# Two attention layers on one core: layer A's output projection as seven block products at the end, and log-sum rows copied by two engines

## The chip, the cores and the metric

The kernel runs on one core of a Trainium2 chip. The metric is the device time of one execution in microseconds (us). Times are given as the median of several runs. The profile is of one execution.

## The reference

Two independent attention layers, A and B, each with its own input `x` (2048 x 1024), `wqkv` (1024 x 3072) and `wo` (1024 x 1024), 32 heads of 32 columns. The two outputs are concatenated.

```python
# layer A: each query sees 8 keys, two positions apart
off = arange(8) * 2;  idx = pos[:, None] - off[None, :]      # masked where idx < 0
attn = softmax(where(mask, einsum(q, k[idx]) * Dh**-0.5, -1e9));  o = einsum(attn, v[idx])
out_A = o.reshape(2048, 1024) @ A_wo
# layer B: each query sees the 256 positions up to itself
p = softmax(where(mask, q @ k.T * Dh**-0.5, -1e9));  o = p @ v
out_B = o.reshape(2048, 1024) @ B_wo
```

All of it is float32.

## The kernel before, in words

**Units and groups.** Each layer's 2048 rows are cut into four units of 512 rows. Units 0 to 3 are layer B (called dense), units 4 to 7 layer A (windowed; the host splits A's rows into even and odd positions, so that its eight keys are neighbours). A unit has eight groups (`NG`) of four heads, 128 columns each. For each unit there are four kinds of matmul work in the "gemm" stream: `qk_items` (queries and keys of a group, 2 x 8 k-tiles), `v_items` (values, in three parts), and `o_items` (a block of 128 output columns of the projection, 8 k-tiles). The attention of a group comes between: `first`, `log_sum`, `rows`, `second` and `values` for the dense units, `window` for the others.

**Split precision.** Every matmul operand is split into a high part (rounded to the matmul's float32r format) and a low part (the rest), and a product is three matmuls (`TERMS`, L41): high x high, high x low, low x high. So one k-tile is three matmuls of 128x512, a projection block is 8 x 3 = 24, and a unit's projection is 8 blocks, 192 matmuls.

**The stream of operands.** `Stream` (L131) brings weights and activations from DRAM as raw tiles of 128x1024 float32 (512 KB). There are `NRAW` = 3 raw buffers. POOL's queue issues the loads (L159), in the order of a list of items. `parts` (L195) makes the high part by a copy on ACT or DVE (L201, L204) and the low part by DVE subtracts of 512 columns (L207). Split weights go to three `wpool` tiles, split activations to nine `xpool` tiles. A load is issued when the split of the item three places earlier ends. The matmul items call `split_to` at fixed k-tiles to ask for the next split.

**What sets the order.** All instructions are written out in an order decided while the kernel is built: a `Clock` (L44) keeps for each engine when it would be free by the planner's own durations, callbacks are put off to such times (`defer`), and the loop at L1060 always issues the item that is ready first: row items ("a"), second passes ("2"), first passes ("1"), or gemm. Engines then run their own instructions strictly in that order and wait on semaphores.

**The parts that the change touches.**
- The plan (L243 to L254): units 1 to 7 carry the eight `o` blocks of the unit before, two ahead of each of the groups 2 to 5 (`O_SLOTS`); the eight blocks of unit 7 stand at the end, the first four with their last k-tile put off (`TAIL`, L1038).
- `finish` (L817): the attention output of a group (PSUM, 128x512) is copied to a high part on ACT (L822) and a low part on DVE (L826), into one of ten `opool` tiles, where the projection reads it (L645).
- `o_items` (L622): matmuls at L645, PSUM copied out by ACT or DVE (L536, L539), stored by ACT's queue (L662).
- `log_sum` and `rows` (L878 to L909), dense units only: minus the log of each row's sum, for 128 queries x 16 (head, query block) pairs, is split and transposed by one matmul with the identity (L896), 32x128 into PSUM. `spread` then makes four tiles of 32x512, one for each head, by DVE multiplies with a broadcast mask `pick` of 32x16 (L902). They go to rows 96 to 127 of the query tile, and the second pass (L940) waits for them.
- `constants` (L305): POOL builds masks and `pick` (two selects at L322) before it issues its first load.

The PSUM ring of the gemm stream, `rg`, has three banks.

## Time and profile before

| what | us |
|---|---|
| median of 3 runs | 1831.32 |
| lowest, highest | 1831.26, 1832.84 |
| span of the profiled execution (first to last instruction) | 1830.6 |
| median less that span, taken as what lies around it | 0.7 |
| TensorE (PE) busy | 1807.8 |
| VectorE (DVE) busy | 1202.9 |
| ScalarE (ACT) busy | 889.4 |
| GpSimd (POOL) busy | 394.4 |

How to read it: a group row gives the line, engine and operation, output and input names, shape and count, then busy time, mean ns of one, and the engine's idle time just before it with what ended it. PEld is TensorE's weight load, which runs beside its matmuls. Matmuls overlap in the pipeline, so that the mean ns of one is longer than the step from one to the next. A row of the windows view gives, for a stretch of time, its length, then each engine's busy time with its count of instructions, the granted TensorE clock, the mean busy share of the 16 DMA engines, and GB/s. "To landing" is from a DMA's issue to its last byte.

### The profile page before, as it was taken

What the parts mean: (1) busy time and instruction counts of PE and PEld (TensorE: products, weight loads), DVE (VectorE), ACT (ScalarE), POOL (GpSimd) and SP (SyncE); (2) the same over time, 40 slices, a digit from 0 to 9 for tenths busy, and PEclk for the clock granted to TensorE, in tenths of its full rate; (3) what the DMA queues carried; (4) which work ended last, traced back from release to release, by engine and by line L of the source; (5) the groups of instructions that cost most, each with busy time, mean ns of one, the idle gap of its engine ahead of it and who ended that gap; (6) DMA issues with size and microseconds to landing.
All of it is one profiled execution on the core that took longest, in us unless ns stands there. A gap on an engine that the chain in (4) does not pass through costs nothing.

```text
span 1830.6 us, 38331 instructions
## 1 busy us (share of the span) xinstructions
PE 1807.8 (99%) x14826; PEld 1477.5 (81%) x14826; DVE 1202.9 (66%) x2694; ACT 889.4 (49%) x2254; POOL 394.4 (22%) x926
## 2 busy tenths in 40 slices
PE   9999999999999999999999999999999999999998
PEld 7787777888778888788887788888888788888887
DVE  6677886768867669777777564655547445655463
ACT  5556466565655655656555343433425234423331
POOL 3322323233242324332233200110001000100000
PEclk9999999999999999999999999999999999999999
DMA  8455665545656456455554343444334443534432
GB/s 242 121 138 139 176 164 150 170 121 160 164 155 164 136 151 183 125 157 141 141 142 130 110 135 116 152 143 130 119 115 143 133 138 108 162 107 128 127 104 83
DMA packets 109141, 257.43 MB, mean 141 GB/s; under 512 B 14496, under 2 KB 29856, under 8 KB 108960
## 3 DMA queue, kind: packets, MB, share of 16 engines
q0 software_dynamic: 41760, 152.06, 28.1%
q1 hardware_dynamic: 56832, 83.00, 17.6%
q10 hardware_dynamic: 10368, 19.93, 3.0%
q8 instruction: 117, 1.92, 0.5%
q14 instruction: 64, 0.52, 0.1%
HBM read 164.63 MB, written 23.07 MB: 103 GB/s over the span
## 4 chain that ended last, share of the span: by engine, by line
PE 92%; DVE 4%; DMA 2%; ACT 2%; issue 1%; SPq 0%; ACTq 0%; POOL 0%; DVEq 0%; POOLq 0%
PE g L518 37%; PE g L645 19%; PE g L583 17%; PE s L940 5%; PE s L857 5%; PE o L987 5%; PE s L711 2%; PE o L774 2%; DMA raw<-xs 1%; DVE w L207 1%; DVE s L862 1%; ACT s L867 0%; DMA qst<-nat 0%; DMA pbuf<-nat 0%; DVE x L207 0%
## 5 line engine op out<-in xcount | busy, mean ns | idle before, releaser
L518 PE MATMUL g<-x,w 128*128 128x512 f32 x3072 | 770.2, 394 | 3.8 <-DVE nm L729 2.4
L518 PEld LDWEIGHTS g<-x,w 128*128 128x128 f32 x3072 | 566.3, 189 | 114.2 <-issue 8.3
L583 PE MATMUL g<-w,x 128*128 128x256 f32 (+1 forms) x2304 | 391.9, 320 | 0.9 <-issue 0.7
L207 DVE TENSOR_TENSOR w<-raw,w 128x512 fp32r<-128x512 f32 x516 | 338.6, 698 | 52.0 <-ACT w L201 44.8
L583 PEld LDWEIGHTS g<-w,x 128*128 128x128 f32 x2304 | 332.3, 190 | 29.2 <-DVE w L207 1.8
L645 PE MATMUL g<-ot,w 128*128 128x512 f32 x1416 | 343.6, 393 | 3.7 <-DVE ot L826 1.8
L867 ACT ACTIVATE s<-s,nm 128x384 f32<-128x384 f32 (+2 forms) x512 | 274.3, 536 | 102.1 <-DVE nm L862 101.8
L862 DVE CUSTOM_DVE_ANT_0 s<-s,mask_d 128x384 f32<-128x384 f32 (+2 forms) x512 | 261.5, 553 | 88.2 <-PE s L857 87.5
L645 PEld LDWEIGHTS g<-ot,w 128*128 128x128 f32 x1416 | 262.4, 188 | 59.3 <-DVE ot L826 3.2
L926 POOL TENSOR_SCALAR_AFFINE_SELECT pbuf<-pbuf 128x128 f32<-128x128 f32 (+1 forms) x606 | 219.8, 391 | 325.1 <-ACT pbuf L947 323.8
L947 ACT ACTIVATE pbuf<-s 128x384 f32<-128x384 f32 (+2 forms) x480 | 202.7, 505 | 72.2 <-PE s L940 70.2
L159 POOL DMA_DIRECT2D raw<-wqk x126 | 68.1, 540 | 457.5 <-DVE w L207 356.3
L204 DVE CAST w<-raw 128x1024 fp32r<-128x1024 f32 x205 | 141.7, 691 | 24.8 <-PE g L518 24.0
L940 PEld LDWEIGHTS s<-qst,kst 128*128 128x128 f32 x704 | 113.0, 188 | 41.2 <-ACT s L867 16.3
L857 PE MATMUL s<-kst,qst 96*128 96x384 f32 (+2 forms) x512 | 142.4, 342 | 0.9 <-ACT s L867 0.6
L940 PE MATMUL s<-qst,kst 128*128 128x256 f32 (+2 forms) x704 | 136.5, 302 | 3.5 <-ACT s L867 3.0
L719 DVE TENSOR_TENSOR band<-s,near 128x160 f32<-128x160 f32 x128 | 32.4, 315 | 158.0 <-PE s L711 158.0
L536 ACT COPY ost<-g 128x512 f32<-128x512 f32 x54 | 31.7, 587 | 207.1 <-PE g L645 200.4
L857 PEld LDWEIGHTS s<-kst,qst 96*128 96x128 f32 x512 | 93.4, 189 | 26.2 <-issue 4.7
L826 DVE TENSOR_TENSOR ot<-o,ot 128x512 fp32r<-128x512 f32 x64 | 44.0, 688 | 101.6 <-ACT ot L822 101.4
L867 ACT ACTIVATION_READ_ACCUMULATOR s<-s,nm 128x1 f32 x512 | 105.3, 206 | 0.0
L159 POOL DMA_DIRECT2D raw<-wo x64 | 34.2, 534 | 304.2 <-DVE w L207 260.2
(77 smaller groups left out, 1298.6 us busy)
## 6 DMA issues: line engine op xcount, KB each, us to landing
raw<-wqk POOLq DMA_DIRECT2D x126, 512.0 KB, 4.3
raw<-wv POOLq DMA_DIRECT2D x72, 512.0 KB, 5.1
raw<-wo POOLq DMA_DIRECT2D x64, 512.0 KB, 4.1
qst<-nat SPq DMA_DIRECT2D x96, 256.0 KB, 5.3
kst<-nat SPq DMA_DIRECT2D x96, 256.0 KB, 5.6
raw<-xs POOLq DMA_DIRECT2D x28, 512.0 KB, 4.6
outs<-ost ACTq DMA_DIRECT2D x56, 256.0 KB, 2.3
kst<-halo SPq DMA_DIRECT2D x72, 128.0 KB, 4.5
```

What stands on the lines that cost most here:

```text
L159: (self.nc.scalar if early else self.nc.gpsimd).dma_start(raw if len(ap.shape) == 2 else raw.rearrange("p (a b) -> p a b", a=2), ap)
L204: nc.vector.tensor_copy(t[:, 0, :], raw)
L207: nc.vector.tensor_tensor(t[:, 1, c:c + 512], raw[:, c:c + 512], t[:, 0, c:c + 512].bitcast(F32), op=ALU.subtract)
L518: nc.tensor.matmul(h["ps"], h["w"][:, a, k * P:(k + 1) * P], xt[u][k][:, b, :], start=(k == 0 and i == 0), stop=(k == NK - 1 and i == 2))
L583: nc.tensor.matmul(ps, xt[u][kw * g + k][:, a, p0:p0 + P], h["w"][g][:, c, k], start=(first and t == 0 and half == 0), stop=(last and t == 2),
L645: nc.tensor.matmul(h["ps"], w[:, a, c:c + P], ot[u, k][:, b, :], start=(k == 0 and i == 0), stop=(k == NK - 1 and i == 2))
L857: nc.tensor.matmul(ps[:, :n], q[0:96, j, b * P:(b + 1) * P], kk[0:96, j, c0:c1], start=True, stop=True)
L862: nc.vector.tensor_tensor_reduce(ps[:, :n], ps[:, :n], mask[:, cut:full], scale=-1.0, scalar=BIG, op0=ALU.add, op1=ALU.min, accum_out=nm)
L867: nc.scalar.activation(ps[:, :n], ps[:, :n], AF.Exp, bias=nm, scale=-1.0, accum_out=sm)
L926: nc.gpsimd.affine_select(w, w, pattern=[[0, m], [step, n]], compare_op=ALU.is_ge, fill=0.0, base=base, channel_multiplier=chan)
L940: nc.tensor.matmul(ps[:, i * n:(i + 1) * n], kk[:, j, 256 + kb * P:256 + (kb + 1) * P], q[:, j, q0:q0 + n], start=True, stop=True)
L947: nc.scalar.activation(w, ps[:, :pack * n].rearrange("p (j n) -> p j n", j=pack), AF.Exp)
```

## The change

**Layer A's projection.** The units are taken in pairs (4 and 5, 6 and 7). With the two units as row blocks 1 and 2 of the left matrix, the halves of its columns as column blocks, and `wo` cut into 2 x 2 blocks of 512 x 512, the product of 2 x 2 blocks is formed from seven block products instead of eight. Each product has 4 output blocks of 4 k-tiles, 48 matmuls (L769).

- `finish` in units 4 to 7 copies the attention output to one plain tile on ACT (L1027), and SP stores it to DRAM (`od`, L1032).
- Sums and differences of blocks are made in the background: of the weights (`td`) after unit 3's last projection block, of the attention outputs (`sd`) when groups 4 to 7 of the second unit of a pair end. A task loads 2 x 512 KB on SP, does four DVE operations of 128x512, and stores 2 x 512 KB on SP. There are 4 weight tasks and 8 output tasks.
- All 14 products stand at the end of the gemm stream. Each has four items in the `Stream`: two of activations (`od` or `sd`), two of weights (`wo` or `td`).
- Each product's blocks are copied (first product, ACT) or added (DVE, L787) into running sums in SBUF; the results are stored from ACT's queue in the second, fifth, sixth and seventh product, those of the second and fifth through the one `ost` tile.
- The projection blocks of unit 3 (layer B) are spread over units 4 and 5, four in each (`O_LATE`). No projection stands in units 6 and 7.
- The ten `opool` tiles become a shared pool of ten tiles for attention outputs, background sums and running sums.

**Log-sum rows.** The split values are written with a stride into a zeroed tile `turn`, four matmuls (L1124) put query block b at columns 128b of PSUM, and each of the four copies is then one multiply with a per-row scalar, `pick` being 32x4. Each copy goes to ACT or DVE, whichever the planner has free first. `pick` is built by 32 selects of one column.

The core of the diff:

```diff
-    plan += [("o", U - 1, n) for n in range(NG)]
+    plan += [("p", u, i) for u in range(DU, U, 2) for i in range(7) if u > DU or i not in O_AT.values()]
+PRODUCTS = (("11", "11"), ("12", "21"), (0, 3), (2, 2), ("22", 1), (3, 0), (1, "22"))
+O_LATE = {4: {2: (0, 1), 3: (2, 3)}, 5: {2: (4, 5), 3: (6, 7)}}
...
+        def run(n, k):
+            if k == 0:
+                h["ps"], h["b"] = rg.take()
+            w, x = held["t", u, i, n // 2][0], held["s", u, i, k // 2][0][k % 2]
+            c = S * (n % 2) + P * k
+            for t, (a, b) in enumerate(TERMS):
+                nc.tensor.matmul(h["ps"], w[:, a, c:c + P], x[:, b, :], start=(k == 0 and t == 0),
+                                 stop=(k == 3 and t == 2))
+            if k == 1:
+                at = where["p", u, i, "t", 1]
+                more_w = [kind for kind, _ in st.items[at + 1:at + 1 + (n + 1 if n else 0)]]
...
+            if i == 0:
+                nc.scalar.copy(a, ps)
+            elif i == 1:
+                e = add(o, a)
+                store(0, 0, o, e)
...
+            elif i == 5:
+                e = add(c, c)
+                store(1, 1, c, e)
+                e = add(a, a)
...
+        if u >= DU:
+            o = slot(2 + hg % 2)[:, :S]
+            nc.scalar.copy(o, h["o"])
+            def store():
+                nc.sync.dma_start(od[u][:, s, :], o)
...
-            nc.tensor.matmul(ps[0:32, 0:P], hl.rearrange("p a b -> p (a b)"), cst["ident"], start=True, stop=True)
+            for b in range(4):
+                nc.tensor.matmul(ps[0:32, b * P:b * P + P], turn[:, 32 * b:32 * b + 32].bitcast(F32R), cst["ident"],
+                                 start=True, stop=True)
...
-                    nc.vector.tensor_tensor(q[96:P, j, :].rearrange("p (b s) -> p b s", s=P),
-                                            ps[0:32, None, 0:P].to_broadcast([32, 4, P]),
-                                            cst["pick"][0:32, 4 * j:4 * j + 4, None].to_broadcast([32, 4, P]), op=ALU.mult)
+                    if ck.ends("act", 0.62, ck.now) <= ck.ends("dve", 0.61, ck.now) + SPREAD:
+                        nc.scalar.activation(q[96:P, j, :], ps[0:32, :], AF.Copy, scale=cst["pick"][:, j:j + 1])
+                    else:
+                        nc.vector.tensor_scalar(q[96:P, j, :], ps[0:32, :], cst["pick"][:, j:j + 1], None, op0=ALU.mult)
...
-        for row in (0, 16):
-            nc.gpsimd.affine_select(pick, pick, pattern=[[-1, 16]], ...)
+        for row in range(0, 32, 4):
+            for b in range(4):
+                c = row // 4 % 4
+                nc.gpsimd.affine_select(pick[:, c:c + 1], pick[:, c:c + 1], pattern=[[0, 1]], ...)
+        nc.gpsimd.memset(turn, 0.0)
```

## The prediction

> **What bounds the kernel now.** I read the page's shares first, then the stretches of each stage, then the chain of work at the end.

> ```profile
> span 1830.6 us, 38331 instructions
> PE 1807.8 (99%) x14826; PEld 1477.5 (81%) x14826; DVE 1202.9 (66%) x2694; ACT 889.4 (49%) x2254; POOL 394.4 (22%) x926
> PE 92%; DVE 4%; DMA 2%; ACT 2%; issue 1%; SPq 0%; ACTq 0%; POOL 0%; DVEq 0%; POOLq 0%
> ```

> TensorE is busy 1807.8 of 1830.6 us, and the chain that ended last is TensorE for 92%. Only 22.8 us of the span are open to anything that is not TensorE work. Stage by stage (TensorE busy is the second number; then its count, weight loads, DVE, ACT, POOL, granted clock, DMA share, GB/s):

> ```profile
> 0.00:60.00 60.00, 56.84 (x233) 44.44 (x234) 39.68 (x101) 33.32 (x81) 18.55 (x49) 0.97 0.69 202
> 60.00:1030.00 970.00, 961.49 (x5895) 776.47 (x5896) 722.79 (x1854) 562.84 (x1627) 298.63 (x737) 1.00 0.54 148
> 1030.00:1780.00 750.00, 743.68 (x8436) 619.94 (x8431) 422.26 (x710) 281.99 (x526) 75.08 (x138) 1.00 0.43 130
> 1780.00:1827.00 47.00, 45.76 (x269) 36.63 (x267) 18.19 (x31) 10.70 (x20) 2.12 (x4) 1.00 0.26 84
> ```

> TensorE idles 3.2 us in the start, 8.5 in the dense layer, 6.3 in the windowed one, 1.2 at the end, and 3.6 after its last matmul. So the change is worth what it takes from the matmul stream, less the waits it puts in.

> **The matmuls removed.** Layer A's projection is 4 units x 8 blocks x 24 = 768 matmuls of 128x512 before. After it is 2 pairs x 7 products x 48 = 672 of the same shape. The pace stands in the chain's last pieces:

> ```profile
> 1805.13 21.77 PE g L645 x96
> 1826.90 0.02 issue
> 1826.92 0.58 ACT pbuf L536
> ```

> 96 matmuls took 21.77 us, 0.2268 each, and 96 is the number that goes: **-21.8 us**. They are taken from the engine that bounds, so nothing hides the gain. After the last matmul an eviction and a store remain, as before (0.69 instead of 0.58 us): 0.

> **The log-sum rows.** The 32 calls of `rows` make four matmuls instead of one, 96 more. `spread` shares 128 copies between two engines: the built order has 62 on DVE and 66 on ACT.

> ```profile
> 157.64 0.47 PE s L857 x4
> 160.33 0.06 PE s L896
> L896 PE MATMUL s<-ident,hl 128*32 128x128 f32 x32 | 7.1, 222 | 3.6 <-DVE hl L888 3.6
> L902 DVE TENSOR_TENSOR qst<-s,pick 32x512 fp32r<-32x512 f32 x128 | 79.3, 676 | 9.9 <-PE s L896 9.4
> ```

> In the chain one such matmul costs 0.06 us (its 222 ns are pipelined length). Four other 128-column matmuls in a row cost 0.47, or 0.12 each. I take 0.06, the row of the same shape: 96 x 0.06 = **+5.8 us**, at most 96 x 0.12 = 11.5. Nothing hides it. The gate of the second pass comes earlier: four DVE copies in a row were 2.7 us, two on each engine are 1.4. DVE loses 66 x 0.676 = 45 us of its 723 in the dense stage and ACT gains about as much on 563. That helps only where TensorE idles, 8.5 us in all. I take **-2 us**, between -5 and +3 (ACT is also in the softmax chain).

> **The start.** `pick` is now built by 32 selects of one column instead of two of 16, and one more memset follows, ahead of POOL's first load.

> ```profile
> 1.49 0.45 POOL L322 TENSOR_SCALAR_AFFINE_SELECT pick<-pick 32x16 f32<-32x16 f32 x2
> 10.02 1.19 POOL L159 DMA_DIRECT2D raw<-wqk  x2 [0.30 <-issue]
> 19.72 0.69 DVE L459 SCALAR_TENSOR_TENSOR nat<-g,nat 128x512 fp32r<-128x512 f32 x1 [4.46 <-ACT nat L455]
> 20.32 0.68 DVE L204 CAST w<-raw 128x1024 fp32r<-128x1024 f32 x1
> raw<-wqk POOLq DMA_DIRECT2D x126, 512.0 KB, 4.3
> ```

> At 0.19 to 0.225 us each, 30 more selects and a memset are 6 to 7 us. The first load goes out at 16 to 17 instead of 10.0, and with 4.3 us to landing arrives at 20.3 to 21.3. DVE split it at 20.3 anyway, since it stood behind L459. So the cover is used up: **+0.5 us**, between 0 and 1.5.

> **The end, where the new waits are.** Each product takes 48 x 0.2268 = 10.9 us and needs four raw tiles of 512 KB, two of activations and two of weights. Before, a block of 5.4 us needed one. The tiles pass through the same three raw buffers, POOL's load queue, ACT's high parts and DVE's low parts:

> ```profile
> q0 software_dynamic: 41760, 152.06, 28.1%
> outs<-ost ACTq DMA_DIRECT2D x56, 256.0 KB, 2.3
> L207 DVE TENSOR_TENSOR w<-raw,w 128x512 fp32r<-128x512 f32 x516 | 338.6, 698 | 52.0 <-ACT w L201 44.8
> L207 DVE TENSOR_TENSOR x<-raw,x 128x512 fp32r<-128x512 f32 x70 | 47.1, 692 | 16.6 <-ACT x L201 15.3
> L201 ACT CAST w<-raw 128x1024 fp32r<-128x1024 f32 x52 | 54.1, 1047 | 10.9 <-PE g L583 6.4 <-ACT ost L536 2.7 <-DVE band L731 0.7
> L201 ACT CAST x<-raw 128x512 fp32r<-128x512 f32 x31 | 17.8, 618 | 22.7 <-DMA raw<-xs 19.9 <-DVE x L204 2.6
> L539 DVE COPY pbuf<-g 128x512 f32<-128x512 f32 x2 | 1.4, 690 | 6.6 <-PE g L645 6.5
> ```

> DVE per product: 8 subtracts of 0.69 and 4 adds from PSUM (nearest row: the copy from PSUM, 0.69) are 8.3 us, and in the sixth product, with 8 adds, 11.0 of 10.9. The bank ring lets an add come 5.4 us late, so that passes. ACT's copies are 4 x 0.62 + 2 x 1.05 = 4.6.

> The three buffers are the tight loop. Counted from a product's start, splits for the next product are asked for after 18, 30 and 42 matmuls: 4.1, 6.8 and 9.5 us. The first activation tile's low parts end at 4.1 + 0.62 + 2 x 0.69 = 6.1 and free its buffer. The last weight tile is then loaded into that buffer and lands L later. It is split in 1.05 + 1.40 and frees the buffer at 8.55 + L. The following product's first weight tile goes there, and is split at 11.0 + 2L. TensorE needs it at 2 x 10.9 = 21.8. So L may be 5.4 us, and 5.2 with about 0.1 for each of four hand-overs. Beyond that **each product waits L - 5.2**.

> What L will be depends on the traffic:

> ```profile
> raw<-wo POOLq DMA_DIRECT2D x64, 512.0 KB, 4.1
> 1811.00:1816.00 5.00, 5.00 (x24) 4.14 (x23) 0.83 (x2) 0.19 (x1) 0.00 (x0) 1.00 0.14 52
> 700.00:740.00 40.00, 38.78 (x260) 29.54 (x259) 33.70 (x88) 23.53 (x65) 14.96 (x30) 1.00 0.72 204
> DMA to landing us min/median/max: 4.0/5.5/6.9
> 90.00:100.00 10.00, 10.00 (x79) 8.80 (x78) 8.26 (x28) 7.16 (x28) 0.55 (x1) 1.00 0.83 202
> DMA to landing us min/median/max: 4.8/4.8/4.8
> 20.00:44.00 24.00, 24.00 (x111) 19.34 (x109) 19.32 (x50) 14.15 (x33) 3.43 (x5) 1.00 0.99 263
> DMA to landing us min/median/max: 4.3/7.0/9.3
> ```

> A load holds the 16 engines 0.281 x 1830.6 / 290 = 1.77 us; a 256 KB store 0.14 x 5 = 0.7. A product without stores uses 7.1 of 10.9 us (65%). The second, fifth, sixth and seventh also store four blocks: 9.9 of 10.9 (91%). Loads land in 4.8 to 5.5 us at shares of 0.83 and 0.72, and in 7.0 at 0.99. At 91% I take 5.6, nearer to the former: 0.4 us in each of seven such products. The first pair is worse. While products 0 to 2 run, 12 loads (21.2), 4 stores (2.8), the last two sum tasks (each 2 x 1.77 in and 2 x 1.4 out, 12.7) and two attention stores (1.4) want 38.1 of 32.7 us. Of the 5.4 too many I charge 3, since the splits run a product ahead. Together **+6 us**; the bounds are 0 (L of 4.1 to 5.2) and 14 x (7.0 - 5.2) = 25.

> [...]

> **The windowed units.** Units 6 and 7 lose the projection blocks that stood between windows; unit 4 and 5 keep the dense layer's. From a window's scores to its values TensorE must have other work:

> ```profile
> 1737.13 1.32 PE L711 MATMUL s<-pbuf 32*32 32x40 f32 x128
> 1752.97 1.18 PE L774 MATMUL o<-wide,vbuf 128*32 128x8 f32 x40
> ```

> This one took 14.6 us after its scores. In the new order 48 matmuls and the next scores stand between, 12.1 us. But the windows lose 32 low parts of 0.69 on DVE, and the weight splits of layer A's blocks move to the end, so the vector chain is less disturbed. SP gets 32 attention stores and the sums' 48 transfers, in front of which seat copies for later windows wait. I take **+1 us** on the 6.3 now lost, between -3 and +10.

> **Sum.** 1830.6 - 21.8 + 5.8 - 2 + 0.5 + 6 + 1 = 1820.1. The median is 0.7 above the profiled span, so **1820.8 us**. About 0.2% (3.7 us) is what a measurement of this kernel can tell from no change.

> **Rivals.** The first row is for the third of them: least, median and greatest ns of POOL's load issues in the whole run.

> ```profile
> L159 POOL DMA_DIRECT2D raw<-wo x64: 528/528/651, 234.2 to 1797.6; - x64
> ```

> 1. *The raw-buffer loop takes the gain back* (slower). Without the end's waits the net gain is 16.5 us. Over 14 products that is 1.18 each, so it decides at L = 6.4. At the 7.0 of the start it costs 25 us: 1840. For it: 91% traffic in bursts. Against: stores come evenly spaced, and 4.8 at a share of 0.83. 0.11.
> 2. *No waits at the end.* Landing stays at 4.1 to 5.2, and +6 falls away: 1815. The median of 4.1 speaks for it, the 91% against. 0.20.
> 3. *The load queue is held up by DVE.* Each load's issue waits for a two-input subtract, 0.69 us. L is then 5.5 without stores and 6.3 with: 0.3 x 6 + 1.1 x 7 instead of 2.8, 7 us more, 1828. If it waits for both halves, 1834. [...] The row is against it: the issues take 528 ns in the median and 651 at most, with DVE two thirds busy. 0.06.
> 4. *The windows of units 6 and 7 run dry.* Half of the 2.5 us between 14.6 and 12.1, in some ten windows: 12 us, 1832. 0.07.
> 5. *The row matmuls don't pipeline.* 96 x 0.222 = 21 instead of 5.8: 1836. 0.04.
> 6. *The change doesn't do what it says.* The built order holds 672 product matmuls and 128 row matmuls, so this leaves only an unseen block: 0.02, slower.

> **How the numbers follow.** The forecast has 0.50 (1816 to 1827). Faster: forecast 0.50, rival 2 0.20, the lighter rival 3 and part of rival 1 below its point 0.07, together 0.77. Within 0.2%: rival 4 and the heavier rival 3, 0.08. Slower: rivals 1, 5, 6 and the worst of 4, 0.15. The range is 1810 (rival 2 with -5 in the dense stage) to 1836 (the row matmuls at 0.12 with 13 us at the end, or rival 5); some 0.13 is left out, most of it rival 1.

> **What would show it.** The product group (672 matmuls) should keep 0.2268 us in unbroken runs. Idle TensorE in the last 160 us should be about 6 us beyond its final 3.6, put down to DVE's low part of w at product starts, mostly in the first three products. The loads landing there should have a median of 5 to 5.6. POOL's first load should be at 16 to 17 us and row matmuls should cost 0.06 in the chain. The forecast is wrong if the windows of units 6 and 7 show idle TensorE above 10 us, or if loads take over 6.4 us.

## The result, and the profile after

The changed kernel takes 1900.35 us (median of 4 runs, 1896.20 to 1900.99), the kernel before 1831.29 beside it: a ratio of 1.037, 95% interval 1.036 to 1.039. The forecast was 1820.8, with a range of 1810 to 1836. The time went up by 69 us, where some 10 less were expected.

The profiled execution after is the shortest of the four (1896.20). Its page, with span and busy times:

```profile
span 1894.5 us, 38848 instructions
PE 1832.6 (97%) x14826; PEld 1481.9 (78%) x14826; DVE 1226.6 (65%) x2727; ACT 971.4 (51%) x2366; POOL 424.1 (22%) x979
```

TensorE now idles 61.9 us, before 22.8. The changed kernel has 21.8 us less product work and 5.8 more for the row matmuls, and yet TensorE is busy 24.8 us longer: part of its work ran at a lower clock. The stages of after, with the columns as in the rows of before (TensorE's granted clock is the third number from the end):

```profile
0.00:60.00 60.00, 50.00 (x199) 38.67 (x199) 35.06 (x87) 29.18 (x69) 22.18 (x66) 0.94 0.66 193
60.00:1070.00 1010.00, 987.24 (x5954) 787.85 (x5955) 690.49 (x1802) 607.93 (x1696) 306.93 (x745) 0.99 0.50 141
1070.00:1712.00 642.00, 631.39 (x7954) 525.52 (x7956) 388.56 (x658) 269.66 (x507) 65.91 (x118) 0.99 0.53 169
1712.00:1891.00 179.00, 163.94 (x726) 129.89 (x722) 112.46 (x182) 64.62 (x95) 29.07 (x51) 0.96 0.70 228
```

A clock of 0.99 over 1010 us looks harmless, and is 10 us or more. To see it I cut both traces into stretches of 2 us, and took from each its idle time (length less busy) and its clock loss (busy time by one less the granted clock). What is left I call work. (In the run e11 below, the lengths of the trains of matmuls give 16.9 us lost to the clock between 306 and 620 us; reckoned in this way from the granted clock, 0.93 up to 480 us and 0.95 behind it, they are 16.7.) The stages end at landmarks: the first first pass, the last second pass, the last window scores, the end. Each entry is idle / clock loss, in us:

| stage | length before, after | before | after | more |
|---|---|---|---|---|
| start | 31.1, 38.2 | 3.0 / 1.6 | 9.9 / 1.7 | 7.0 |
| dense | 995.3, 1028.7 | 8.7 / 0.0 | 22.8 / 14.6 | 28.7 |
| windows | 750.2, 641.8 | 6.3 / 0.0 | 8.5 / 3.3 | 5.5 |
| end | 54.0, 185.8 | 4.8 / 0.0 | 20.7 / 5.8 | 21.7 |
| sum | 1830.6, 1894.5 | 22.8 / 1.6 | 61.9 / 25.4 | 62.9 |

So 39.1 us more are idle and 23.8 are lost in clock. Work is almost as before (1807.2 against 1806.1), where 16.0 less were due. The other 17 us lie in time that counts as busy, for which the views list no wait. Four places carry the loss. The two largest:

**The dense stage.** The copies of the log-sum rows in after's timeline (start, duration, engine, operation, and in brackets the idle time before it with what ended it):

```profile
413.86 0.40 PE L1124 MATMUL s<-ident,turn 128*32 128x128 f32 x4
...
414.10 2.36 PE L650 MATMUL g<-w,x 128*128 128x256 f32 x18
414.30 0.74 DVE L1136 TENSOR_SCALAR qst<-s,pick 32x512 fp32r<-32x512 f32 x1 [1.00 <-PE s L1124]
415.08 0.68 ACT L1133 ACTIVATE qst<-s,pick 32x512 fp32r<-32x512 f32 x1 [2.55 <-DVE qst L1136]
415.79 0.74 DVE L1136 TENSOR_SCALAR qst<-s,pick 32x512 fp32r<-32x512 f32 x1 [0.75 <-ACT qst L1133]
...
416.57 0.68 ACT L1133 ACTIVATE qst<-s,pick 32x512 fp32r<-32x512 f32 x1 [0.81 <-DVE qst L1136]
...
417.30 1.03 PE L1172 MATMUL s<-qst,kst 128*128 128x128 f32 x6 [0.38 <-ACT qst L1133]
```

The four copies run one behind the other, 414.30 to 417.25: 2.95 us, not 1.4. While one engine copies the other stands, and six matmuls of the second pass wait for the last copy (0.38 us). The two groups, with idle time before them and what ended it:

```profile
L1136 DVE TENSOR_SCALAR qst<-s,pick 32x512 fp32r<-32x512 f32 x62 | 45.8, 743 | 45.6 <-ACT qst L1133 27.3 <-PE s L1124 18.1
L1133 ACT ACTIVATE qst<-s,pick 32x512 fp32r<-32x512 f32 x66 | 43.6, 675 | 93.1 <-DVE qst L1136 81.2 <-PE s L1124 11.5
```

ACT stood 81.2 us for DVE's copies and DVE 27.3 for ACT's. In the timeline each copy starts 0.03 to 0.04 us after the other engine's copy before it has ended, and that copy is named as what released it.

**The end.** What waited behind 1712 us (total us, times, longest), TensorE first, then DVE:

```profile
PE g L769 <- DVE ost L787: 12.1, 6, 6.2
```

```profile
DVE ost L787 <- DMA outs<-ost: 30.6, 11, 7.3
```

And the longest of them in the timeline:

```profile
1741.51 0.69 DVE L787 TENSOR_TENSOR ost<-g,r 128x512 f32<-128x512 f32 x1 [2.23 <-DMA outs<-ost]
...
1750.67 0.69 DVE L787 TENSOR_TENSOR ost<-g,r 128x512 f32<-128x512 f32 x1 [7.26 <-DMA outs<-ost]
...
1751.50 2.04 PE L769 MATMUL g<-x,w 128*128 128x512 f32 x4 [6.22 <-DVE ost L787]
1751.77 1.66 ACT L214 CAST x<-raw 128x512 fp32r<-128x512 f32 x3 [13.02 <-DVE ost L787]
```

There is one `ost` tile. An addition into it waits until the store before it has landed. The PSUM bank stays taken, and TensorE stops. ACT, whose queue holds the next store's issue in front of the casts, stands 13.0 us.

### The profile page after: what moved, and what is told of

Read it like the earlier page. It is cut to its first block, busy times and chain, and to the rows that moved or that the text cites. A ratio compares the mean times of both kernels' runs of the same rounds, so it can differ in the third digit from the quotient of the medians.

```text
span 1894.5 us, 38848 instructions
## 1 busy us (share of the span) xinstructions
PE 1832.6 (97%) x14826; PEld 1481.9 (78%) x14826; DVE 1226.6 (65%) x2727; ACT 971.4 (51%) x2366; POOL 424.1 (22%) x979
## 5 line engine op out<-in xcount | busy, mean ns | idle before, releaser
L582 PE MATMUL g<-x,w 128*128 128x512 f32 x3072 | 775.6, 397 | 7.0 <-ACT x L214 2.7
L582 PEld LDWEIGHTS g<-x,w 128*128 128x128 f32 x3072 | 572.4, 190 | 122.9 <-issue 5.8
L650 PEld LDWEIGHTS g<-w,x 128*128 128x128 f32 x2304 | 336.9, 192 | 28.7 <-issue 2.7
L1092 ACT ACTIVATE s<-s,nm 128x384 f32<-128x384 f32 (+2 forms) x512 | 274.2, 536 | 105.1 <-DVE nm L1087 103.9
L1158 POOL TENSOR_SCALAR_AFFINE_SELECT pbuf<-pbuf 128x128 f32<-128x128 f32 (+1 forms) x604 | 226.7, 407 | 291.4 <-ACT pbuf L1179 288.7
L710 PE MATMUL g<-r,w 128*128 128x512 f32 x768 | 196.7, 396 | 0.0
L769 PE MATMUL g<-x,w 128*128 128x512 f32 x672 | 162.0, 401 | 14.3 <-DVE ost L787 12.1
L769 PEld LDWEIGHTS g<-x,w 128*128 128x128 f32 x672 | 128.6, 194 | 47.5 <-issue 15.3
L710 PEld LDWEIGHTS g<-r,w 128*128 128x128 f32 x768 | 141.7, 188 | 28.4 <-issue 0.4
L1082 PE MATMUL s<-kst,qst 96*128 96x384 f32 (+2 forms) x512 | 149.6, 347 | 11.5 <-ACT s L1092 5.0
L1172 PE MATMUL s<-qst,kst 128*128 128x256 f32 (+2 forms) x704 | 143.9, 312 | 12.4 <-ACT qst L1133 7.5
L217 DVE CAST w<-raw 128x1024 fp32r<-128x1024 f32 x183 | 125.9, 688 | 32.6 <-PE g L582 19.9
L1082 PEld LDWEIGHTS s<-kst,qst 96*128 96x128 f32 x512 | 94.5, 190 | 40.2 <-ACT s L1092 13.2
L214 ACT CAST w<-raw 128x1024 fp32r<-128x1024 f32 (+1 forms) x77 | 79.5, 1037 | 61.6 <-DMA raw<-wo 19.9
L170 POOL DMA_DIRECT2D raw<-wv x72 | 46.2, 642 | 276.0 <-DVE w L220 172.1
## 6 DMA issues: line engine op xcount, KB each, us to landing
raw<-wqk POOLq DMA_DIRECT2D x126, 512.0 KB, 4.1
raw<-wv POOLq DMA_DIRECT2D x72, 512.0 KB, 4.3
qst<-nat SPq DMA_DIRECT2D x96, 256.0 KB, 3.7
kst<-nat SPq DMA_DIRECT2D x96, 256.0 KB, 4.0
raw<-wo POOLq DMA_DIRECT2D x44, 512.0 KB, 4.1
raw<-xs POOLq DMA_DIRECT2D x28, 512.0 KB, 6.0
outs<-ost ACTq DMA_DIRECT2D x48, 256.0 KB, 2.3
```

The costliest lines, as they stand in the source:

```text
L217: nc.vector.tensor_copy(t[:, 0, :], raw)
L582: nc.tensor.matmul(h["ps"], h["w"][:, a, k * P:(k + 1) * P], xt[u][k][:, b, :], start=(k == 0 and i == 0), stop=(k == NK - 1 and i == 2))
L650: nc.tensor.matmul(ps, xt[u][kw * g + k][:, a, p0:p0 + P], h["w"][g][:, c, k], start=(first and t == 0 and half == 0), stop=(last and t == 2),
L710: nc.tensor.matmul(h["ps"], w[:, a, c:c + P], ot[u, k][:, b, :], start=(k == 0 and i == 0), stop=(k == NK - 1 and i == 2))
L769: nc.tensor.matmul(h["ps"], w[:, a, c:c + P], x[:, b, :], start=(k == 0 and t == 0), stop=(k == 3 and t == 2))
L1082: nc.tensor.matmul(ps[:, :n], q[0:96, j, b * P:(b + 1) * P], kk[0:96, j, c0:c1], start=True, stop=True)
```

## The experiments

Medians, and ratios to the kernel before, measured beside it (1830.7 to 1832.3):

| kernel | us | ratio, 95% interval |
|---|---|---|
| changed kernel | 1900.35 | 1.0357 to 1.0387 |
| e1_two_banks | 1863.54 | 1.0154 to 1.0191 |
| e2_strassen_alone | 1846.08 | 1.0065 to 1.0097 |
| e3_logsum_alone | 1883.68 | 1.0267 to 1.0301 |
| e4_short_pick | 1890.01 | 1.0292 to 1.0351 |
| e6_spread_dve | 1875.28 | 1.0219 to 1.0249 |
| e8_strassen_pbuf | 1834.27 | 0.9996 to 1.0023 |
| e9_all_mended | 1848.23 | 1.0066 to 1.0100 |
| e10_spaced | 1834.16 | 1.0006 to 1.0030 |
| e12_fourth_raw | 1824.35 | 0.9955 to 0.9979 |
| e13_raw_spaced | 1824.40 | 0.9953 to 0.9977 |
| e14_told | 1893.46 | 1.0306 to 1.0361 |
| e15_dve_told | 1874.71 | 1.0205 to 1.0241 |

My theory at the outset: separate waits at the four places, each with clock lost behind it. The rival: one part of the change disturbs the other.

### Each part alone

**e2_strassen_alone** has the log-sum part and `pick` of the kernel before, from the first line to the copies:

```diff
-                hl = turn[:, :132].rearrange("p (b x) -> p b x", x=33)
+                hl = small.tile([P, 2, 16], F32R, tag="hl", name="hl")
...
-            for b in range(4):
-                nc.tensor.matmul(ps[0:32, b * P:b * P + P], turn[:, 32 * b:32 * b + 32].bitcast(F32R), cst["ident"],
-                                 start=True, stop=True)
+            nc.tensor.matmul(ps[0:32, 0:P], hl.rearrange("p a b -> p (a b)"), cst["ident"], start=True, stop=True)
```

> The changed kernel with the log-sum part and the constants of the kernel before (one row matmul, four VectorE products, pick of 32x16 with two selects): the Strassen part alone. Theory: start and dense stage are as before, first first-pass matmul near 31 us and last dense second pass near 1027, so 7 + 33 us less: 1856 to 1864, and what is left above before, 25 to 33 us, lies in the windows and at the end. Rival: the dense stage's loss comes with the Strassen part (dense products moved, tiles shared); then 1880 or more.

Measured: 1846.1, less than either theory gave. The dense stage is as before (996.8 us long, idle 7.7, clock 1.6). So its loss does not come with the projection.

**e3_logsum_alone** is the other half: the kernel before with the changed constants, row matmuls and copies.

```diff
-        pick = cst["pick"] = pickp.tile([32, 16], F32, name="pick")
+        pick = cst["pick"] = pickp.tile([32, 4], F32, name="pick")
...
-                hl = small.tile([P, 2, 16], F32R, tag="hl", name="hl")
+                hl = turn[:, :132].rearrange("p (b x) -> p b x", x=33)
```

> The kernel before with the changed constants and log-sum part alone (32 selects, four row matmuls, copies on two engines from one bank), layer A's projection classical. Theory: start +7 and dense stage +33 as in the changed kernel, nothing after: 1866 to 1874, that is slower than before by itself. Rival: the parts disturb each other, and alone this one costs less than 20 us: under 1852.

Measured: 1883.7, 52 us above before, more than expected; I had left out the matmul work that the dense stage leaves over for the windows. The two parts alone cost 14.6 and 52.2, together 66.8, where the change costs 69. They add up, so the rival falls. Three quarters of the loss is the log-sum part.

### The dense stage

**e1_two_banks** keeps everything but the bank:

```diff
-            ps, bank = rs.take()
+            halves = [rs.take() for _ in range(2)]
             for b in range(4):
-                nc.tensor.matmul(ps[0:32, b * P:b * P + P], ...)
+                ps = halves[b // 2][0]
+                nc.tensor.matmul(ps[0:32, b % 2 * P:b % 2 * P + P], ...)
...
+                    for d in range(2):
+                        ps = halves[d][0][0:32, 0:256]
+                        to = q[96:P, j, 256 * d:256 * d + 256]
+                        if d:
+                            nc.scalar.activation(to, ps, AF.Copy, scale=cst["pick"][:, j:j + 1])
...
+                        else:
+                            nc.vector.tensor_scalar(to, ps, cst["pick"][:, j:j + 1], None, op0=ALU.mult)
```

> The changed kernel, but the four transposed 128-column blocks go to two PSUM banks, two to each, and each engine copies the half that lies in its bank: VectorE four 32x256 copies with columns 0 to 255, ScalarE four with 256 to 511, none of them waiting for the other engine. As many row matmuls as in the changed kernel. Theory: the dense stage's 33 us come from the two engines taking turns at one bank (0.74 + 0.04 + 0.68 + 0.03 us, in series 3.0 us where the prediction had 1.4) and from the clock lost behind the stalls. Then the last dense second pass ends 25 to 34 us earlier than at 1066.9, the stage's idle time and clock loss fall to before's or less, and the time is 1866 to 1876. Rival: the four row matmuls, the turn tile or the Strassen part's tile layout slow the dense stage; then the time stays within 6 us of 1900.

Measured: 1863.5, 36.8 less and a little more than expected. The last second pass is at 1040.3 (26.6 earlier). The dense stage's idle time and clock loss fall to 12.9 and 5.1 us, not to before's 8.7 and 0.0 as expected. Four copies on each engine, and their groups, in this kernel:

```profile
402.60 1.65 DVE L1140 TENSOR_SCALAR qst<-s,pick 32x256 fp32r<-32x256 f32 x4 [0.88 <-PE s L1125]
402.72 1.53 ACT L1137 ACTIVATE qst<-s,pick 32x256 fp32r<-32x256 f32 x4 [1.77 <-PE s L1125]
```

```profile
L1140 DVE TENSOR_SCALAR qst<-s,pick 32x256 fp32r<-32x256 f32 x128 | 52.9, 470 | 21.1 <-PE s L1125 20.9
L1137 ACT ACTIVATE qst<-s,pick 32x256 fp32r<-32x256 f32 x128 | 49.0, 452 | 36.6 <-PE s L1125 36.2
```

Neither engine waits for the other any more, though both still read `pick` and write the same query tile. Only the row matmuls hold them. So it is the shared PSUM bank that made them take turns (81.2 and 27.3 us of waits for each other in after, none listed here). Four copies of 256 columns took 1.5 and 1.7 us here, side by side. The second bank has a price: TensorE's row matmuls now wait 3.9 us (five times) for a bank that ACT's exponentials still read (`PE s L1125 <- ACT s L1092`), a wait that the changed kernel does not have.

**e6_spread_dve.** Are the hand-overs the price, or the length of the series?

```diff
-SPREAD = 0.0
+SPREAD = -99.0
```

> The changed kernel with all four copies of the rows on VectorE (2.97 us in series by 0.743 each) and none on ScalarE; row matmuls, selects and projection as in the changed kernel. Theory: what costs is not the 3.0 us of the series but that each engine's queue stands behind the other at every hand-over, so that ScalarE's exponentials and VectorE's mask steps behind the copies start late. Without hand-overs the dense stage is as before plus the row matmuls (5.8) and 0.3 us a step (9): its last second pass at 1046 to 1054, the time 1880 to 1888. Rival: the length of the series and the dearer copies are the cost; then the series is as long as it was, and the time stays within 6 us of 1900 or rises, VectorE having 64 copies more.

Measured: 1875.3, 25 less, but the last second pass is at 1062.1 and the dense stage idles 22.6 us, as with hand-overs (22.8). So my theory, that the idle time is the price of the queues behind the hand-overs, fails. The four copies in a row are 2.72 us in its timeline, so the hand-overs had added only 0.2 us to the series. What fell is the clock loss (14.6 to 4.9), and time that counts as busy (the table below).

**e14_told** and **e15_dve_told.** The order of instructions is fixed by a planner that reckoned with 0.61 and 0.62 us for a copy and two engines side by side. Both kernels tell it the truth (e14 takes turns, j odd on ACT; e15 keeps `SPREAD` at -99, so that all copies go to DVE):

```diff
-                    if ck.ends("act", 0.62, ck.now) <= ck.ends("dve", 0.61, ck.now) + SPREAD:
+                    if j % 2:
...
-                        ends.append(ck.use("act", 0.62, ck.now))
+                        last = ck.use("act", 0.72, last)
...
-                        ends.append(ck.use("dve", 0.61, ck.now))
+                        last = ck.use("dve", 0.78, last)
```

> The changed kernel with the four copies still from one bank and in turn, VectorE, ScalarE, VectorE, ScalarE, but with the planner told so: 0.78 and 0.72 us each, one behind the other (3.0 us), where it had reckoned with two engines side by side (1.25 us). Theory A, the order: second passes were put into TensorE's queue 1.7 us too early, and TensorE, which can't pass them, stood; told, it is given other matmuls meanwhile, the dense stage's idle time falls from 22.8 to 10 to 16 us, the clock loss from 14.6 to under 6, and the time is 1867 to 1882. Theory B, the queues: whatever the plan, each engine stands at every hand-over with its own work behind it, and the time stays within 6 us of 1900.

> The changed kernel with all four copies on VectorE, as in e6_spread_dve (1875.3), and with the planner told 0.78 us for each (it took 0.61 there; the copies take 0.743). Theory A, the order: the second pass was planned 0.5 us too early, so some of the 22.6 us of idle time in the dense stage goes: 1862 to 1871. Theory B: the idle time there comes from VectorE's load (64 copies more than the changed kernel), which is as it was: 1872 to 1879.

Measured: 1874.7 in e15, as theory B had it, and 1893.5 in e14, 6.9 below the changed kernel and nearer to B than to A. TensorE's waits in the dense stage, first of after, then of e14:

```profile
PE s L1172 <- ACT qst L1133: 7.5, 19, 0.8
PE s L1082 <- ACT s L1092: 5.0, 6, 1.2
PE s L1172 <- DVE qst L1136: 3.9, 7, 1.5
PE s L1124 <- DVE turn L1115: 2.0, 1, 2.0
```

```profile
PE s L1124 <- DVE turn L1115: 9.3, 4, 2.9
PE s L1082 <- ACT s L1092: 4.8, 5, 1.3
PE s L1172 <- DVE qst L1136: 1.9, 2, 0.9
...
PE s L1172 <- ACT qst L1133: 0.8, 3, 0.3
```

Told the truth, the second pass no longer waits for the copies (11.4 us become 2.7), and TensorE waits for the split rows instead (2.0 become 9.3). The dense stages compared with before's 995.3 us, with the matmuls that were put off to the windows (57 of 512 columns and 6 of 256 in after, 42 of 512 in e1) charged at 0.2268 each, those of 256 columns at half of it:

| kernel | longer | put off | loss | of it idle | of it clock |
|---|---|---|---|---|---|
| changed | 33.4 | 13.6 | 47.0 | 14.1 | 14.6 |
| e14_told | 37.6 | -2.7 | 34.9 | 11.5 | 9.7 |
| e6_spread_dve | 29.4 | 0.0 | 29.4 | 13.9 | 4.9 |
| e15_dve_told | 28.5 | 0.7 | 29.2 | 8.5 | 6.7 |
| e1_two_banks | 6.8 | 9.5 | 16.3 | 4.2 | 5.1 |
| e2_strassen_alone | 1.5 | 0.0 | 1.5 | -1.0 | 1.6 |

Of the 47, some 12 go when the planner is told (but e14 loses them again in the windows, with 14.8 us idle and 11.0 of clock there). Another 19 go when the copies run side by side from two banks. How much of these 19 is the hand-overs and how much the length of the series is not separated: with a series of 2.72 us on one engine (e15), 6 of them go, and there VectorE does 64 copies more than in e14. The last 16 stay: 5.8 for the row matmuls, the rest idle time and clock. Nor is the shared bank all of it. e6 has, as before, all copies on VectorE, in 2.72 us where before has 2.48, and still loses 29.4, of which the row matmuls are 5.8. Of the other 24, 13.9 are idle time and 4.9 clock: TensorE waits there for ACT's exponentials (`PE s L1082 <- ACT s L1092` 8.4 us, in before 0.6) and for the split rows (7.7, before 3.6). Why these come later than in before is not shown. And before's 8.7 us of idle time in this stage, of which the forecast took 2 off, grew in every variant of the log-sum part, least in e1 (12.9).

### The start

**e4_short_pick** builds the same mask in four instructions:

```diff
-        for row in range(0, 32, 4):
-            for b in range(4):
...
-                nc.gpsimd.affine_select(pick[:, c:c + 1], ...)
+        for base, step, chan in ((0, -4, 1), (3, 4, -1)):
+            nc.gpsimd.affine_select(pick8, pick8, pattern=[[step, 8]], compare_op=ALU.is_ge, ...)
+        nc.gpsimd.tensor_tensor(pick, pick8[:, 0:4], pick8[:, 4:8], op=ALU.add)
```

> The changed kernel with the same pick of 32x4 built in one memset, two selects and one addition in the place of one memset and 32 selects. Theory: the 32 selects hold GpSimd for 8.5 us (0.227 us each and the gaps), and with it the first load on its queue (issued at 19.7 us, before 10.0), so the first first-pass matmul comes 5 to 8 us earlier than at 38.2 and the time is 1892 to 1895. Rival: the start is held by the wqk halves on ScalarE's queue, which landed 1.9 us late too; then the gain is under 2 us.

POOL's timeline, first after, then e4:

```profile
1.49 6.81 POOL L387 TENSOR_SCALAR_AFFINE_SELECT pick<-pick 32x1 f32<-32x1 f32 x26
8.56 1.71 POOL L387 TENSOR_SCALAR_AFFINE_SELECT pick<-pick 32x1 f32<-32x1 f32 x6 [0.27 <-POOL pick L387]
...
19.69 1.22 POOL L170 DMA_DIRECT2D raw<-wqk  x2 [0.32 <-issue]
```

```profile
1.49 0.43 POOL L385 TENSOR_SCALAR_AFFINE_SELECT pick<-pick 32x8 f32<-32x8 f32 x2
2.00 0.19 POOL L388 TENSOR_TENSOR pick<-pick 32x4 f32<-32x4 f32 x1
...
10.58 1.23 POOL L170 DMA_DIRECT2D raw<-wqk  x2 [0.32 <-issue]
```

Measured: first first pass at 31.6 instead of 38.2, 6.6 us. The median fell by 10.3, but its runs spread from 1884.3 to 1895.7, so the start's own 6.6 is the better number.

### The end

**e8_strassen_pbuf** is e2 with one line changed:

```diff
-                o = stp.tile([P, S], F32, tag="ost", name="ost")
+                o = pbuf[:, n, :S]
```

> The Strassen part alone (1846.1) with the sums of products 1 and 4 written to four slices of pbuf, idle by then, in the place of the one ost tile: an addition no longer waits for the store before it. Theory: the idle time put down to ost (10.6 us, and 2 to 4 of clock behind it) goes: 1830 to 1837. Rival: the loop through the raw buffers, which the prediction held for the cost of the end, is next in line behind the stores (loads of 3.8 to 5.6 us through three buffers) and takes its place; then the gain is under 5 us, and the idle time is put down to the low parts of w and to casts that wait for loads.

Measured: 1834.3, 11.8 less than e2. TensorE's waits behind the last scores, first e2, then e8:

```profile
PE g L765 <- DVE ost L783: 10.6, 5, 6.5
PE g L765 <- DVE r L783: 2.9, 3, 2.3
PE g L765 <- ACT w L214: 2.2, 2, 2.0
```

```profile
PE g L765 <- ACT w L214: 5.4, 3, 3.1
PE g L765 <- DVE r L783: 1.3, 3, 0.6
```

The wait for `ost` is gone. The cast of weights, which in turn waits for `raw<-td` and `raw<-wo`, is next in line, as the rival said, but with 3.2 us more only; the gain is not under 5.

**e12_fourth_raw** tests whether that is the loop through the raw buffers:

```diff
+            if self.loaded >= self.wide and (self.loaded - self.wide) % 4 == 0:
+                raw = self.fourth
...
+    st.wide, st.fourth = where["p", DU, 3, "s", 0], more[:, 2048:3072]
...
-            self.ck.defer(end, lambda n=i + m + NRAW + 1 if i < NRAW else max(2 * NRAW + m, i + NRAW + 1): self.load_to(n))
+            more_raw = int(i >= self.wide)
+            self.ck.defer(end, lambda n=i + m + NRAW + 1 if i < NRAW else max(2 * NRAW + m, i + NRAW + 1 + more_raw): self.load_to(n))
```

> As e8_strassen_pbuf, with a fourth raw buffer (the last third of pbuf) in rotation from the fourth product of the first pair on, and loads asked for one item earlier from there; the sums of products 1 and 4 lie in the first two thirds. Theory: what is left at the end (172.0 us behind the last scores, where 672 matmuls are 152.4) is the loop through the raw buffers: waits put down to casts of w (5.4 us) that waited for raw<-td, raw<-wo. With four buffers 3 to 6 us of it go: 1828 to 1831. Rival: the loads are late because the 16 DMA queues are busy (share 0.76 at the end, before 0.24), not because they start late; then the time stays within 1.5 us of 1834.

Measured: 1824.4, beyond the expected gain: 9.9 less than e8 by the medians, and 7.9 by the two ratios to the kernel before (1.0010 and 0.9967; they were measured at different times). It is **0.33% faster than the kernel before** (ratio 0.9967). One wait is left behind the last scores in e12:

```profile
PE g L771 <- ACT w L219: 2.4, 1, 2.4
```

The loads took no less from issue to landing (in the median 5.3 us, 5.0 in e8; `raw<-wo` 5.7 and 5.1). So what went is the wait for a free buffer: the loop was the limit, and not the traffic.

**e10_spaced** and **e13_raw_spaced** take the sums' additions apart (e13 all but the last pair's):

```diff
-            for to, x, y, op in ops:
-                nc.vector.tensor_tensor(...)
-            ck.defer(e, put)
+            to, x, y, op = ops[0]
+            nc.vector.tensor_tensor(...)
+            ops[:] = ops[1:]
+            ck.defer(e + 2.0 if ops else e, add if ops else put)
```

> As e8_strassen_pbuf, but a sum task's four VectorE additions go out one by one, 2.6 us apart by the plan, in the place of four in a row (2.9 us). Theory: in the windows the additions hold VectorE ahead of the low parts of x and w, so raw buffers come free late and a weight load with them (at 1343 to 1349 the PE waited 2.9 us in three waits, and the clock fell to 0.5); spaced, these waits go with their clock, and the time is 4 to 10 us under e8's. Rival: the windows' loss comes from the sums' transfers (DMA share 0.69 where before had 0.43) and from stalls in which no releaser is seen; then the time is within 2 us of e8's.

> As e12_fourth_raw, with the additions of the weight sums and of the first pair's sums spaced as in e10_spaced, those of the last pair in a row. Theory: spacing took 4.5 us from the windows (630.4 to 625.9) and gave 5 to the end (172.0 to 177.0), because the last pair's sums came later; with the last pair's left in a row the 4.5 us stay: 3 to 5 us under e12. Rival: windows and end move against each other whatever is spaced; then within 1.5 us of e12.

Measured: 1834.2 and 1824.4, the same as e8 and e12. In the profiled runs the windows are 4.5 us shorter in e10 than in e8, and the end is 5.0 longer; nothing is left of it in the whole. So the additions in a row are not what the kernel loses by, and this theory falls. In e8 the windows idle 12.0 us instead of 6.3, and 6.0 us of them are stalls to which the trace gives no releaser ("issue"; before 1.7). Their cause stays open.

**e9_all_mended** has two banks, the short `pick` and `pbuf` in the changed kernel.

> The changed kernel with the three repairs together: two banks for the rows, the short pick, pbuf for the sums of products 1 and 4. Theory, adding single effects: 1863.5 with two banks, less 7 for the start, less 11 to 16 for the stores: 1838 to 1847, so still slower than before, by the row matmuls, the waits in the windows and what is left at the end. Rival: repaired waits hand their time to each other; then 1850 or more.

Measured: 1848.2, a little above the expected range: 15.4 us of idle time at the end are left (the loop) and 15.1 in the dense stage.

### The price of a gap

**e11_gaps** and **e16_gaps_scattered** put trains of 50 to 63 matmuls in front of the kernel before, with gaps of known length (the loop of e16; e11 has ten trains of 60 for each gap):

```diff
+        for k in GAPS:
+            for r in range(14):
+                for _ in range(k):
+                    nc.scalar.copy(idle, ps)
+                for i in range(50 + r):
+                    nc.tensor.matmul(ps, idle[:, :P], idle, start=(i == 0), stop=(i == 49 + r))
```

> The kernel before with a stretch put in front of its loads' first use: five groups of ten trains of 60 matmuls of 512 columns, each train waiting for one, two, three, four or five ScalarE copies behind the train before it, so that the PE idles some 0.9, 1.5, 2.1, 2.8 and 3.4 us between trains of 13 us. It measures the price of an idle gap in granted clock. Theory: each gap of about 1.6 us or more can cost up to 2 us more behind it (clock 0.5 to 0.6 over 4 us), but not every time, because in the changed kernel and in the kernel before gaps of 2 us were followed by both: in the groups with 2.1 us and more between a fifth and all of the ten gaps are followed by a lower clock, in the group with 0.9 none. Rival: the length alone decides, at one threshold; then each group has all or none.

> As e11_gaps, with gaps of 1.35, 1.97, 2.58, 3.20 and about 3.8 us, fourteen of each, and trains of 50 to 63 matmuls so that the gaps do not come at one period. In e11 none of ten gaps of 0.73, none of ten of 1.35, seven of ten of 1.97, four of ten of 2.58 and none of ten of 3.20 us were followed by a slow train (15.2 to 15.5 us where the others took 13.9). Theory: a gap is weighed in fixed stretches of time, so that its place in them decides, and equal periods (17.09 us with 3.20) put all gaps at one place; scattered, some half to three quarters of the gaps of 1.97 us, and more of the longer ones, are followed by a lower clock, none of 1.35, at 1.3 to 1.7 us each. Rival: long gaps really cost nothing, as in e11; then none of those of 3.20.

The measurement is in the timeline of e16 (start, length of the train, and its gap in brackets), here with the granted clock of one stretch below (third number from the end):

```profile
240.72 12.10 PE L1062 MATMUL s<-qst 128*128 128x512 f32 x52 [1.96 <-ACT qst L1060]
254.79 13.95 PE L1062 MATMUL s<-qst 128*128 128x512 f32 x53 [1.97 <-ACT qst L1060]
```

```profile
254.79:258.79 4.00, 4.00 (x12) 3.19 (x13) 0.00 (x0) 0.00 (x0) 0.00 (x0) 0.68 0.00 0
```

One matmul more should cost 0.23 us, but behind a gap of the same length one train takes 1.85 more than the next shorter: 1.6 us of clock. The last line shows it in the granted clock: 0.68 over the first 4 us of that train. Over the other 9.95 us of it the clock was 0.96, and in a train behind a gap of 1.35 us (205.0 to 209.7 us) 1.00. By these, 4.0 x 0.32 + 9.95 x 0.04 = 1.7 us were lost.

None of thirteen gaps of 1.35 us were followed by this, nine of fourteen of 1.97, nine of 2.58, ten of 3.20 and all of 3.8, at 1.3 to 2.9 us each. (The first train of the run is left out: it is slow, but so are the ten matmuls before it, at 0.46 us each.) In e11 none of ten of 3.20 had been, all at one period. So the length alone does not decide, and the rival falls. That the place in time does can be read from both runs together. Fold the starts of the gaps at a period of 3.41 us: for each run and each of the lengths 1.97, 2.58 and 3.20, those that were followed by a lower clock lie in one unbroken part of the period and the others in the rest, without an exception. At every period between 2 and 8 us that differs from it by more than 0.02, at least four gaps lie on the wrong side.

## Why the prediction was wrong, step by step

- **The matmuls removed, -21.8: right.** The group has 672, and in e12 the work is 20.3 us less than before.
- **The row matmuls, +5.8: right.** 0.24 us for four in the timeline above (413.86 to 414.10). The group's busy time was 13.1 us.
- **"Two on each engine are 1.4", -2: the step that failed most.** The series took 2.95 us, and the stage lost 47, of which two banks gave back 31 (e1). I set the copies side by side because they were on two engines, and did not ask what both read. They read one PSUM bank, and waited 81.2 and 27.3 us for each other; from two banks (e1) no such wait is listed, and four copies on each took 1.65 and 1.53 us. By 2.95 us against before's series (2.48 in the timeline; my 2.7 was four times the mean of one) the step would have had no gain to count.
- **The start, +0.5: 7.1.** The selects took 0.23 us each on the mean, as I had it at most, but their two rows in the timeline, gaps between them included, are 8.5 us, 8.1 more than the row of before. The eight selects of `near` behind them took 5.53 us, before 4.37. So the load went out at 19.69, not at 16 to 17. My cover, DVE's split at 20.3, did not hold: in after DVE waits for that load, and TensorE's first pass comes late, as their timelines show:

```profile
23.87 0.69 DVE L217 CAST w<-raw 128x1024 fp32r<-128x1024 f32 x1 [2.06 <-DMA raw<-wqk]
...
38.23 0.63 PE L1082 MATMUL s<-kst,qst 96*128 96x128 f32 x4 [3.52 <-DMA kst<-nat]
```

- **The end, +6: right in kind, and less than half of the 21.7 us.** The loop through the raw buffers was there: with a fourth buffer (e12) 8 to 10 us less than without (e8), clock included. But it did not work as I had it, a wait of 0.4 us in each of seven products with loads of 5.6. In after the loads landed in 4.8 us in the median (3.7 to 7.6), which by my own slack of 5.2 costs nothing. In e8 the two long waits for a cast of w, 2.0 and 3.1 us, stand at product starts at 1676 and 1705 us, where I had charged 3 us for the first pair's traffic, and the last 288 matmuls, six products, run without a wait listed. What I left out is the single `ost` tile, 11.8 us by e2 and e8: I had counted its stores as traffic, not as waits.
- **The windows, +1: 5.5,** 2.2 idle and 3.3 in clock.
- **The clock was not in the sum at all, and is 23.8 us.** I counted idle time as its own price. The rows of the kernel before gave no sign of more: its gap of 2.0 us at 178 us was followed by a clock of 1.00. Such a gap can pass by its place in time: in e16 five of fourteen gaps of 1.97 us did.
- **The rivals.** The first (the loop, slower than before) is the mechanism of a part of the end. None of the others happened: the issues of the sums' loads took 528 to 547 ns on POOL, those of `raw<-wo` there 717 to 731, 0.2 us more than before where the third rival asks for 0.69, and the row matmuls did pipeline. No rival held the mechanism that cost most.

What stays open: why the dense stage of e6, without any turns, loses 24 us beyond its row matmuls; some 12 us in the changed kernel's dense stage that count as busy; and the windows' stalls without a releaser. Of the 12, most lie in the two passes: their groups are 7 us longer each at the same count, of which 2.4 and 2.5 are clock.

## What to carry to other kernels

Copies shared between two engines took turns here while both read one PSUM bank (2.95 us for the four, 81.2 and 27.3 us of waits for each other), and ran side by side from two (e1, 1.65 and 1.53 us): ask which bank each reads, before counting half the time. (In e1 both still read `pick` in SBUF.) For a kernel whose TensorE is 99% busy, price each new wait of 2 us or more at that wait and some 1.6 us of clock, for about half of them (39 of the 72 gaps of 1.97 to 3.20 us in e11 and e16). And count for each new loop the buffers on its way out as well as on its way in: the store's one tile cost 11.8 us here, the loads' three 8 to 10.
